# Sums by fours of the second batch's queries and keys, moved from TensorE to GpSimd

## The chip, the core and the metric

The kernel runs on one core of a Trainium2 chip. The metric is the device time of one execution in microseconds (us); the median of three runs of the kernel before is 896.6 us (895.24 to 897.03).

## What is computed

Attention for 4 batches of 8 heads, 576 tokens and 64 elements a head, followed by two dense layers over the 2304 tokens. Cut to what matters:

```python
q_d = q.reshape(B, H, Sd, factor, D).mean(axis=3)      # factor 4: means over groups of four tokens
k_d, v_d = ...                                         # the same for k and v
out_up = np.repeat(sm_attn(q_d, k_d, v_d), factor, axis=2)
mask = np.abs(pos[:, None] - pos[None, :]) < factor    # a band of 7 keys a query
out_local = softmax(where(mask, scale * q @ k.T, -1e9)) @ v
x = out_up + out_local                                 # 2304 x 512
h = np.maximum(x @ w_in, 0.0);  x = h * h @ w_out      # 512 -> 2048 -> 512
h = x @ w_in2;  out = softplus(h) @ w_out2             # 512 -> 2048 -> 512
```

## The kernel before

**Work.** The tokens of the MLP are cut into five blocks of 8, 6, 8, 8 and 6 times 64 (`BLOCKS`). A step is one chunk of 128 hidden units of one layer for one block. `hidden` (L1015) issues 12 matmuls of a step into the tile `ph`; ScalarE and VectorE make the activation and split it in a high and a low part, `gh` and `gl` (L351); `outputs` (L1069) issues the second 12 matmuls, into `y`. All products are made from two rounded parts, so there are three matmuls for each. A block's steps can start when its attention output has been split into `xh` and `xl` (L351). The first layer begins with steps 0 to 9 (block 0, hidden chunks 0 to 7; the first two chunks are taken in two halves of 256 tokens), and step 10 is the first of block 1.

**Weights.** `weight_job` turns each half chunk (the input half, or the output half) into two rounded parts. The half arrives by DMA in a ring of three `raw` tiles; ScalarE makes `f` and `r` (L401, L404), VectorE runs L407, L410 and L414 on `f`, one of the two copies the high part `w` (L338 or L340), and VectorE writes the low part (`w<-f,w`, L351). So the order of the writes `w<-f,w` is the order in which half chunks become usable: the 14th is the output half of step 8, the 15th the input half of step 9. Later layers get the same chunks back from memory through GpSimd's queue (`weight_again`, L445).

**Attention.** `local` does the band for one group of 64 tokens (scores `lsc`, transposes `lpp`, products `lav`, results `lt`). `pooled` does the pooled attention of one pair of heads: sums by fours of queries and keys into `qkd`, scores `psc` (L638), a softmax, transposes `ppp`, sums of v (`vd`), products `ppo`. Four pairs make a batch. For batch 0 the sums by fours are a VectorE reduction (L627). For batch 1 (`SUMS_ON_PE`) the host stores the tokens so that the four of a group lie 144 columns apart, and TensorE adds them with four matmuls against the identity (`pqk`, L617); ScalarE or VectorE then copies the sums from PSUM to `qkd`. The loaded queries and keys stand in a ring of two `in` tiles. Batch 1's pooled attention and groups are needed by block 1, so they run among the first steps.

**What sets the order.** Every piece of work is a generator that yields the engine it wants, an assumed duration and what it needs. `Order.run` picks, again and again, the piece that can start first by these assumed durations, and issues its instructions. So the order on every engine is fixed when the program is built, each engine works through its queue in that order, and only semaphores decide the times. A change of one piece's engine or assumed duration can reorder all queues. `keep_busy` (L981) adds small matmuls (`idle`) wherever this planner sees TensorE without work, until step 4 is planned.

Of the kernel before, what the change touches and what calls it, by code (L numbers as in the profile page):

```python
# [13 lines left out]
ALU = mybir.AluOpType  # L14
# [8 lines left out]
FCT = 4  # L23
SP = S // FCT
# [31 lines left out]
for run in RUNS:  # L56
    b = run[1] + run[0] * NB
# [12 lines left out]
POOLED = [(-20, -17), (-2.5, -2), (31, 48), (60, 78)]  # L70
LOCAL = [(-17, -13), (-0.5, 5), (12, 58), (62, 86), (74, 92)]
BY_TWOS = [2, 3]
SUMS_ON_PE = [1]

U_MLP, U_WEIGHTS, U_ATT, U_DIRECT = -2, -0.5, 1, 20
AHEAD = 10
# [195 lines left out]
def t_act(n):  # L272
    return 0.09 + n * 0.84e-3


def t_dve(n):
    return 0.066 + n / 960


def t_either(n, fast=False):  # L280

    return t_act(n), t_dve(n / 2 if fast else n)
# [3 lines left out]
def fused_kernel(ctx: ExitStack, tc: tile.TileContext, lq, lk, lv, dqk, dv, cdmask, pqk, pv, wts, cmask, cident, out):  # L286
    nc = tc.nc
    act, dve, pe, sp = nc.scalar, nc.vector, nc.tensor, nc.sync
# [8 lines left out]
    def ring(pool, tag, shape, bufs, dtype=F32):  # L297
        return Ring(lambda name: pool.tile(shape, dtype, tag=tag, name=name, bufs=bufs), bufs)

    ident = const.tile([128, 128], F32, name="ident")  # L300
# [15 lines left out]
    r_s = ring(att, "s", [128, 2 * SP], BUFS["s"])  # L316
    r_e = ring(att, "e", [128, 3 * SP], BUFS["e"])
    r_vd = ring(att, "vd", [KH, 2, 128], BUFS["vd"])
    r_pt = ring(att, "pt", [KH, 2 * 288], BUFS["pt"])
    r_n = ring(att, "n", [128, 16], BUFS["n"])  # L320
# [13 lines left out]
    either = ("act", "dve")  # L334

    def copy(out, in_):
        if order.chosen == "act":
            act.activation(out=out, in_=in_, func=AF.Copy)  # L338
        else:
            dve.tensor_copy(out=out, in_=in_)  # L340
# [20 lines left out]
    def step_start(s):  # L361
        return started if s < 0 else hidden_at[s]
# [140 lines left out]
    def take_for(r, kind, at):  # L503
        return first_bufs.get((kind, at)) or r.take(kind)

    def room(r, kind, at):
        return [] if (kind, at) in first_bufs else [r]
# [80 lines left out]
    def bank(choices, name):  # L588
        r = min((c for c in choices if c.at is not None), key=lambda c: c.at)
        return r.take(name)  # L590
# [8 lines left out]

    def pooled(b, hp, banks, ev, pace):  # L600

        on_pe = b in SUMS_ON_PE
        two = b * NP + hp

        def halves():
            return ev.buf.tile.rearrange("p (a x) -> p a x", a=2)[:, :, :S]

        if hp == 0:
            yield None, 0.0, r_up
            ups[b] = r_up.take("up")  # L610
        if on_pe:
            t = yield "pe", 1.95, ev, pace, banks, r_s, r_e, r_n
            sums = bank(banks, "pqk")
            x4 = halves().rearrange("p a (j g) -> p a j g", j=FCT)
            src = sums.tile[:, :2 * SP].rearrange("p (a g) -> p a g", a=2)
            for k in range(FCT):
                pe.matmul(src, ident, x4[:, :, k], start=(k == 0), stop=(k == FCT - 1))  # L617
            qk, e, n = r_s.take("qkd"), r_e.take("pe"), r_n.take("pn")
            ev.buf.free = t
            t = yield either, t_either(288)  # L620
            copy(qk.tile, sums.tile[:, :2 * SP])
            sums.free = t
        else:
            t = yield "dve", t_dve(1152), ev, pace, *room(r_s, "qkd", two), *room(r_e, "pe", two), r_n
            qk, e, n = take_for(r_s, "qkd", two), take_for(r_e, "pe", two), r_n.take("pn")
            x4 = halves().rearrange("p a (g j) -> p a g j", j=FCT)
            dve.tensor_reduce(out=qk.tile.rearrange("p (a g) -> p a g", a=2), in_=x4, axis=AX.X, op=ALU.add)  # L627
            if b:
                ev.buf.free = t
            else:  # L630
                used_once(t, ev.buf)

        t = yield "pe", 0.5, banks
# [6 lines left out]
        t = yield "dve", t_dve(432)  # L640
        nm, sm = n.tile[:, :3], n.tile[:, 4:7]
        dve.tensor_reduce(out=nm, in_=sc3, axis=AX.X, op=ALU.max, negate=True)
        t = yield "dve", 0.07
        k = 1.0 / (FCT * FCT * D ** 0.5)
        dve.tensor_scalar(out=nm, in0=nm, scalar1=k, scalar2=None, op0=ALU.mult)
        t = yield "act", 1.05
# [5 lines left out]
        t = yield "dve", 0.07  # L652
        dve.tensor_scalar(out=sm, in0=sm, scalar1=1e-9, scalar2=float(FCT), op0=ALU.add, op1=ALU.mult)
        t = yield "dve", 0.09
        dve.reciprocal(out=sm, in_=sm)
        t = yield either, (0.92, t_dve(432))
        times(e3, sm)
        n.free = t
        for a in range(2):
            t = yield ("pe", 0.33, banks, r_pt) if a == 0 else ("pe", 0.33, banks)  # L660
# [8 lines left out]
            t = yield either, t_either(288)  # L669
# [4 lines left out]
        t = yield "dve", t_dve(1024), ev.v, r_vd  # L674
# [4 lines left out]
        t = yield "pe", 0.66, banks  # L679
        po = bank(banks, "ppo")  # L680
        for a in range(2):
            pt4 = pt3[:, a, :].rearrange("p (i h q) -> p h i q", i=3, h=2)
            for h in range(2):
                pe.matmul(po.tile[64 * h:64 * h + 64, :SP], vd.tile[:, a, 64 * h:64 * h + 64], pt4[:, h],
                          start=(a == 0), stop=(a == 1))
        vd.free = pt.free = t
        t = yield either, t_either(144)
# [91 lines left out]
    def used_once(t, *bufs):  # L779
        for x in bufs:  # L780
            x.left -= 1
            if not x.left:
                x.free = t
# [350 lines left out]
    with tc.manual_schedule():  # L1134
# [6 lines left out]
        for k, ((kind, at, hp, i, s), ev) in enumerate(zip(tasks, arrived, strict=True)):  # L1141
            pace = step_start(int(s) + SPLIT) if s >= 0 else started if i == 0 else up_ready[0]
            banks = every if i == 0 else [r_a]
# [16 lines left out]
def _layout(q, k, v, moe_w_in, moe_w_out, moe2_w_in, moe2_w_out):  # L1160
# [15 lines left out]
    for b in range(B):  # L1176
        for i in range(NBLK):
            g = b * NBLK + i
# [3 lines left out]
            lv[at] = vs[b, i * QB:i * QB + KW].reshape(KW, NP * 128)  # L1182
    pqk = np.zeros((B * NP, 128, 2, QKW), f4)
    pqk[:, :, 0, :S], pqk[:, :, 1, :S] = qt.reshape(B * NP, 128, S), kt.reshape(B * NP, 128, S)
    for b in SUMS_ON_PE:
        x = pqk[b * NP:(b + 1) * NP, :, :, :S]
        x[...] = x.reshape(NP, 128, 2, SP, FCT).swapaxes(3, 4).reshape(x.shape)
    pqk = pqk.reshape(B * NP, 128, -1)
# [3 lines left out]
    for wi, wo in ((moe_w_in, moe_w_out), (moe2_w_in, moe2_w_out)):  # L1192
        a = np.asarray(wi, np.float64).reshape(DM // 128, 128, NF, 128).transpose(2, 1, 0, 3).reshape(NF, 128, 512)
# [47 lines left out]
```

## Time and profile before

| | |
|---|---|
| median of three runs | 896.6 us |
| the profiled execution | 897.16 us |
| its span, first to last instruction | 895.4 us |
| TensorE busy | 884.2 us (99%) |
| VectorE busy | 623.6 us (70%) |
| ScalarE busy | 482.6 us (54%) |
| GpSimd busy | 70.0 us (8%) |
| granted TensorE clock | 1.00 of full speed |

The share of TensorE is an average, and it counts the `idle` matmuls as work. Which engine sets the pace differs by stage, so the stages up to 125 us, in which all of batch 1's sums lie, have to be read by themselves.

### The profile page before, as it was taken

To read this page: it belongs to the slowest core of one execution; us is meant where nothing else is said; L and a number is where in the kernel's file an instruction comes from. 1 tells how busy PE (TensorE), PEld (TensorE's weight loads), DVE (VectorE), ACT (ScalarE), POOL (GpSimd) and SP (SyncE) were. 2 spreads that over 40 slices of the span, in tenths; PEclk is the share of its full clock that TensorE was granted. 3 is DMA by queue.
4 is the path that set the end of the run, shared out by engine and by line. 5 is a ranking of instruction groups with operands and counts; after the bars stand their busy time and mean duration, and the time that the engine had idled before them with its cause. 6 is when DMAs were issued, how large, how long until landed. Compare 5 with 4: busy or idle time off the path is not lost.

```text
span 895.4 us, 13254 instructions
## 1 busy us (share of the span) xinstructions
PE 884.2 (99%) x4908; PEld 763.5 (85%) x4908; DVE 623.6 (70%) x1085; ACT 482.6 (54%) x1051; POOL 70.0 (8%) x136
## 2 busy tenths in 40 slices
PE   8999999999999999999999999999999999999998
PEld 7788899988888788888888888888999888988886
DVE  6999989999999999887888999982111224223222
ACT  4978877757767774552345543532333235444443
POOL 0000000000000000211111111111120110010000
PEclk9999999999999999999999999999999999999999
DMA  9599698859686854796866677636360262223001
GB/s 238 159 320 328 247 356 287 295 167 321 220 260 207 289 197 165 260 296 235 269 216 191 221 269 260 213 101 240 131 222 25 70 209 74 71 94 130 23 1 48
DMA packets 48796, 177.39 MB, mean 198 GB/s; under 512 B 5490, under 2 KB 5874, under 8 KB 48732
## 3 DMA queue, kind: packets, MB, share of 16 engines
q1 hardware_dynamic: 29724, 107.33, 35.7%
q0 software_dynamic: 19008, 69.21, 23.9%
q8 instruction: 39, 0.64, 0.3%
q14 instruction: 25, 0.20, 0.1%
HBM read 138.25 MB, written 38.27 MB: 197 GB/s over the span
## 4 chain that ended last, share of the span: by engine, by line
PE 78%; DVE 10%; DMA 6%; ACT 3%; issue 1%; SPq 0%; ACTq 0%; DVEq 0%
PE y L1069 38%; PE ph L1015 37%; DMA raw<-wts 3%; DMA w_first<-lv 1%; DVE gl L351 1%; DVE f L414 1%; DVE prod L935 1%; DVE f L410 1%; DVE w L351 1%; DVE dsc L906 1%; DMA in<-pqk 1%; DVE g L1038 1%; DVE do L942 1%; ACT f L401 1%; DMA w_first<-pqk 1%
## 5 line engine op out<-in xcount | busy, mean ns | idle before, releaser
L1015 PE MATMUL ph<-xh,w 128*128 128x512 f32 (+2 forms) x1304 | 393.8, 365 | 1.1 <-DVE g L1038 0.9
L1015 PEld LDWEIGHTS ph<-xh,w 128*128 128x128 f32 x1304 | 240.9, 188 | 32.9 <-DVE g L1038 1.8
L1015 PE MATMUL ph<-xl,w 128*128 128x512 f32 (+2 forms) x652 | 237.5, 364 | 0.0
L1069 PE MATMUL y<-gh,w 128*128 128x512 f32 (+2 forms) x656 | 199.6, 366 | 0.0
L1069 PE MATMUL y<-w,gh 128*128 128x512 f32 x576 | 179.2, 392 | 1.0 <-ACT o L338 1.0
L351 DVE TENSOR_TENSOR gl<-g,gh 128x512 fp32r<-128x512 f32 (+2 forms) x163 | 101.8, 625 | 85.3 <-ACT gh L338 84.5
L1015 PEld LDWEIGHTS ph<-xl,w 128*128 128x128 f32 x652 | 122.5, 188 | 15.6
L1069 PEld LDWEIGHTS y<-gh,w 128*128 128x128 f32 x656 | 121.0, 188 | 15.8 <-issue 1.2
L445 POOL DMA_DIRECT2D w<-wdram x132 | 69.8, 532 | 758.9 <-ACT gh L338 351.3
L1069 PEld LDWEIGHTS y<-w,gh 128*128 128x128 f32 x576 | 106.8, 188 | 22.4 <-ACT o L338 1.3
L1069 PE MATMUL y<-gl,w 128*128 128x512 f32 (+2 forms) x328 | 119.3, 364 | 0.0
L338 ACT ACTIVATE gh<-g 128x512 fp32r<-128x512 f32 (+2 forms) x127 | 72.9, 574 | 84.5 <-PE y L1069 49.6
L1038 DVE SCALAR_TENSOR_TENSOR g<-ph,g 128x512 f32<-128x512 f32 (+2 forms) x81 | 50.7, 626 | 90.6 <-ACT g L1036 90.4
L1069 PE MATMUL y<-w,gl 128*128 128x512 f32 x288 | 112.6, 391 | 0.0
L1027 ACT ACTIVATE g<-ph 128x512 f32<-128x512 f32 (+2 forms) x82 | 44.6, 543 | 122.8 <-PE ph L1015 102.9
L1032 ACT ACTIVATE g<-ph 128x512 f32<-128x512 f32 (+2 forms) x81 | 44.4, 548 | 100.8 <-PE ph L1015 91.7
L1069 PEld LDWEIGHTS y<-gl,w 128*128 128x128 f32 x328 | 61.6, 188 | 7.0 <-DVE gl L351 0.2
L1069 PEld LDWEIGHTS y<-w,gl 128*128 128x128 f32 x288 | 54.0, 188 | 11.7
L340 DVE CAST gh<-g 128x512 fp32r<-128x512 f32 (+2 forms) x36 | 14.9, 413 | 62.7 <-PE y L1069 51.8
L401 ACT ACTIVATE f<-raw 128x512 f32<-128x512 f32 x64 | 42.7, 671 | 19.0 <-DMA raw<-wts 8.2
L1030 ACT ACTIVATE g<-g 128x512 f32<-128x512 f32 (+2 forms) x82 | 47.5, 579 | 2.0
L1036 ACT ACTIVATE g<-g 128x512 f32<-128x512 f32 (+2 forms) x81 | 47.3, 584 | 2.2
(115 smaller groups left out, 926.6 us busy)
## 6 DMA issues: line engine op xcount, KB each, us to landing
w<-wdram POOLq DMA_DIRECT2D x132, 512.0 KB, 4.3
raw<-wts SPq DMA_DIRECT2D x64, 512.0 KB
wdram<-w SPq DMA_DIRECT2D x64, 512.0 KB
dqk<-dqk SPq DMA_DIRECT2D x11, 896.0 KB
dv<-dv SPq DMA_DIRECT2D x11, 640.0 KB
in<-pqk SPq DMA_DIRECT2D x12, 579.0 KB
out<-o SPq DMA_DIRECT2D x18, 256.0 KB
pv<-pv SPq DMA_DIRECT2D x12, 288.0 KB
```

Of the source, the lines that this page charges most:

```text
L338: act.activation(out=out, in_=in_, func=AF.Copy)
L340: dve.tensor_copy(out=out, in_=in_)
L351: dve.tensor_tensor(out=out, in0=whole, in1=high.bitcast(F32), op=ALU.subtract)
L401: act.activation(out=f.tile, in_=high.bitcast(F32), func=AF.Abs, scale=REBIAS)
L445: nc.gpsimd.dma_start(out=weights[slot][:, half], in_=wdram[c, half])
L1015: pe.matmul(ph.tile[:, :n], w, y, start=(k == 0), stop=(k == len(prs) - 1))
L1027: act.activation(out=o, in_=h, func=AF.Relu)
L1030: act.activation(out=o, in_=o, func=AF.Square)
L1032: act.activation(out=o, in_=h, func=AF.Abs)
L1036: act.activation(out=o, in_=o, func=AF.Ln, bias=1.0)
L1038: dve.scalar_tensor_tensor(out=o, in0=h, scalar=0.0, in1=o, op0=ALU.max, op1=ALU.add)
L1069: pe.matmul(o, wt, y, start=(begin and k == 0), stop=(end and k == 2))
```

## The change

Batch 1's sums no longer go through TensorE and PSUM. GpSimd adds the second half of the four slices to the first half, in place in the loaded tile (576 elements a partition, line 614 of the changed kernel), and then the second quarter to the first, into `qkd` (288 elements, line 617). The planner is told 1.4 and 0.8 us for the two. The host's layout is the same. Lines behind the diff are numbered three lower in the changed kernel.

```diff
-SUMS_ON_PE = [1]
+ON_POOL = [1]
...
-        if on_pe:
-            t = yield "pe", 1.95, ev, pace, banks, r_s, r_e, r_n
-            sums = bank(banks, "pqk")
-            x4 = halves().rearrange("p a (j g) -> p a j g", j=FCT)
-            src = sums.tile[:, :2 * SP].rearrange("p (a g) -> p a g", a=2)
-            for k in range(FCT):
-                pe.matmul(src, ident, x4[:, :, k], start=(k == 0), stop=(k == FCT - 1))
+        if on_pool:
+            t = yield "pool", 1.4, ev, pace
+            x4 = halves()
+            nc.gpsimd.tensor_tensor(out=x4[:, :, :2 * SP], in0=x4[:, :, :2 * SP], in1=x4[:, :, 2 * SP:], op=ALU.add)
+            t = yield "pool", 0.8, r_s, r_e, r_n
             qk, e, n = r_s.take("qkd"), r_e.take("pe"), r_n.take("pn")
+            nc.gpsimd.tensor_tensor(out=qk.tile.rearrange("p (a g) -> p a g", a=2), in0=x4[:, :, :SP],
+                                    in1=x4[:, :, SP:2 * SP], op=ALU.add)
             ev.buf.free = t
-            t = yield either, t_either(288)
-            copy(qk.tile, sums.tile[:, :2 * SP])
-            sums.free = t
```

Three places of the queues, before and after.

GpSimd's queue of the changed kernel, from its start to the first reloads of weights; the queue before has only the reloads there:

```order
L614 ISA
L614 TENSOR_TENSOR in<-in 128x2x288 x2
L617 TENSOR_TENSOR qkd<-in 128x288 x2
L614 TENSOR_TENSOR in<-in 128x2x288
L617 TENSOR_TENSOR qkd<-in 128x288
L614 TENSOR_TENSOR in<-in 128x2x288
L617 TENSOR_TENSOR qkd<-in 128x288
L445 DMA w_1632<-wdram 128x1024
```

All eight additions stand ahead of the first reload; the second pair's first addition stands ahead of the first pair's second.

VectorE's queue before, from the third `lt` of batch 0 on, where the two orders part (`pn<-psc`: the row maxima of a pair's pooled scores):

```order
L847 TENSOR_TENSOR lt<-lav,up 128x256
L407 TENSOR_SCALAR f<-f 128x512
L847 TENSOR_TENSOR lt<-lav,up 128x256
L410 SCALAR_TENSOR_TENSOR f<-raw,f 128x512
L351 TENSOR_TENSOR xl<-lt,xh 128x4x64
L806 SCALAR_TENSOR_TENSOR ls<-lsc,mask 128x280
L351 TENSOR_TENSOR xl<-lt,xh 128x4x64
L812 TENSOR_REDUCE ln<-ls 128x4
L806 SCALAR_TENSOR_TENSOR ls<-lsc,mask 128x280
L642 TENSOR_REDUCE pn<-psc 128x3
```

and now, from the same instruction:

```order
L844 TENSOR_TENSOR lt<-lav,up 128x256
L340 CAST xh<-lt 128x4x64
L351 TENSOR_TENSOR xl<-lt,xh 128x4x64
L844 TENSOR_TENSOR lt<-lav,up 128x256
L340 CAST xh<-lt 128x4x64
L803 SCALAR_TENSOR_TENSOR ls<-lsc,mask 128x280
L351 TENSOR_TENSOR xl<-lt,xh 128x4x64
L844 TENSOR_TENSOR lt<-lav,up 128x256
L809 TENSOR_REDUCE ln<-ls 128x4
L639 TENSOR_REDUCE pn<-psc 128x3
L351 TENSOR_TENSOR xl<-lt,xh 128x4x64
L642 TENSOR_SCALAR pn<-pn 128x3
```

Batch 0's splits (`xh<-lt`) came to VectorE from ScalarE, and the softmax of batch 1's first pairs moved ahead of the first weights (L407, L410).

TensorE's queue before, from step 8's output matmuls to step 9 (each `y` tile has three rows; `w_1503` is step 8's slot, `w_1635` step 9's):

```order
L981 MATMUL idle<-ident 128x128
L1069 MATMUL y_864<-gh,w_1503 128x512
L1069 MATMUL y_864<-gl,w_1503 128x512
...
L1069 MATMUL y_876<-gl,w_1503 128x512
L1069 MATMUL y_876<-gh,w_1503 128x512
L839 MATMUL lav<-lpt,v 64x64 x8
L1015 MATMUL ph<-xh,w_1635 128x512
```

and now (`w_1555` is step 8's slot, `w_1632` step 9's, `w_78` step 10's):

```order
L1012 MATMUL ph<-xh,w_1555 128x512
L1012 MATMUL ph<-xh,w_1632 128x512
L1012 MATMUL ph<-xl,w_1632 128x512
...
L1012 MATMUL ph<-xh,w_1632 128x512
L1012 MATMUL ph<-xh,w_78 128x384
...
L1012 MATMUL ph<-xh,w_78 128x384
L1066 MATMUL y_857<-gh,w_1555 128x512
```

Step 8's 12 output matmuls now come behind the hidden matmuls of steps 9 and 10.

## Rows read from the trace of the kernel before

**Rows 1.** The page: TensorE's busy time, and GpSimd's in tenths, 40 slices of the span.

```profile
PE 884.2 (99%) x4908; PEld 763.5 (85%) x4908; DVE 623.6 (70%) x1085; ACT 482.6 (54%) x1051; POOL 70.0 (8%) x136
...
POOL 0000000000000000211111111111120110010000
```

**Rows 2.** Windows: stretch, length; busy us (count) by engine; clock, DMA share, GB/s.

```profile
28.70:33.70 5.00, 4.99 (x60) 3.91 (x58) 3.42 (x14) 3.76 (x11) 0.00 (x0) 1.00 0.55 212
33.70:53.70 20.00, 18.07 (x216) 15.04 (x212) 19.80 (x53) 16.25 (x57) 0.00 (x0) 1.00 0.59 192
53.70:70.00 16.30, 16.23 (x145) 14.55 (x146) 14.43 (x34) 12.35 (x40) 0.00 (x0) 1.00 0.97 316
70.00:92.00 22.00, 21.94 (x185) 17.70 (x183) 20.65 (x49) 18.31 (x54) 0.00 (x0) 1.00 1.02 335
92.00:112.00 20.00, 20.00 (x188) 16.37 (x188) 18.38 (x46) 17.83 (x50) 0.00 (x0) 1.00 0.64 231
112.00:896.00 784.00, 776.95 (x3840) 673.84 (x3840) 525.49 (x844) 396.99 (x765) 69.79 (x132) 1.00 0.57 189
```

**Rows 3.** Timeline of VectorE, 107 to 114 us: start us, us, instruction.

```profile
107.40 0.68 DVE L351 TENSOR_TENSOR w<-f,w 128x512 fp32r<-128x512 f32 x1
108.00 0.68 DVE L414 CUSTOM_DVE_ANT_0 f<-f,r 128x1024 uint16<-128x1024 uint16 x1
...
109.88 0.68 DVE L351 TENSOR_TENSOR w<-f,w 128x512 fp32r<-128x512 f32 x1
...
113.89 0.41 DVE L351 TENSOR_TENSOR xl<-lt,xh 128x256 fp32r<-128x256 f32 x1
```

**Rows 4.** Timeline of TensorE, 108 to 115 us.

```profile
108.16 0.39 PE L981 MATMUL idle<-ident 128*128 128x128 f32 x2
108.30 0.49 PE L1069 MATMUL y<-gh,w 128*128 128x512 f32 x1
...
111.88 0.50 PE L1015 MATMUL ph<-xh,w 128*128 128x512 f32 x1
...
114.50 0.56 PE L1015 MATMUL ph<-xh,w 128*128 128x512 f32 x2
```

**Rows 5.** Timeline of TensorE: batch 1's sums, and the scores behind them.

```profile
30.61 2.10 PE L617 MATMUL pqk<-in,ident 128*128 128x288 f32 x8
...
48.09 4.06 PE L617 MATMUL pqk<-in,ident 128*128 128x288 f32 x16
...
53.74 1.69 PE L638 MATMUL psc<-qkd 64*64 64x144 f32 x24 [0.96 <-ACT qkd L338]
...
58.78 2.10 PE L617 MATMUL pqk<-in,ident 128*128 128x288 f32 x8
```

**Rows 6.** Instructions on the tile `pqk`: count; duration ns min/median/max; first and last start.

```profile
L338 ACT ACTIVATE qkd<-pqk x4: 400/410/412, 33.2 to 60.9; 128x288 f32<-128x288 f32 x4
```

**Rows 7.** Timeline of VectorE: the two waits that the sums are behind, in brackets.

```profile
33.37 0.42 DVE L847 TENSOR_TENSOR lt<-lav,up 128x256 f32<-128x256 f32 x1 [1.54 <-PE lav L839]
...
54.74 1.34 DVE L642 TENSOR_REDUCE pn<-psc 128x3 f32<-128x432 f32 x2 [0.97 <-PE psc L638]
```

**Rows 8.** Groups of VectorE by form, 15 to 130 us: count; busy us, mean ns.

```profile
L351 DVE TENSOR_TENSOR xl<-lt,xh 128x256 fp32r<-128x256 f32 x14 | 5.8, 418 | 0.2
...
L351 DVE TENSOR_TENSOR gl<-g,gh 128x512 fp32r<-128x512 f32 x6 | 4.1, 684 | 0.0
...
L340 DVE CAST gh<-g 128x256 fp32r<-128x256 f32 x3 | 0.9, 292 | 0.6 <-ACT g L1030 0.4
...
L340 DVE COPY up<-ppo 128x144 f32<-128x144 f32 x1 | 0.3, 308 | 0.0
```

**Rows 9.** Timeline of SP's queue: the loads of batch 1's third and fourth pairs.

```profile
42.65 0.35 SPq L574 DMA_DIRECT2D in<-pqk  x1
...
50.24 0.33 SPq L574 DMA_DIRECT2D in<-pqk  x1
```

**Rows 10.** The chain that ended last, merged: start us, us, what; one step's output matmuls.

```profile
97.50 2.72 PE y L1069 x12
```

More of the change, by code (lines that the diff above doesn't have):

```diff
@@ L600, in pooled @@
     def pooled(b, hp, banks, ev, pace):
-        on_pe = b in SUMS_ON_PE
+        on_pool = b in ON_POOL
         two = b * NP + hp
@@ L1184, in _layout @@
     pqk[:, :, 0, :S], pqk[:, :, 1, :S] = qt.reshape(B * NP, 128, S), kt.reshape(B * NP, 128, S)
-    for b in SUMS_ON_PE:
+    for b in ON_POOL:
         x = pqk[b * NP:(b + 1) * NP, :, :, :S]
```

## The prediction

> **What bounds the kernel now.** I read the page first: TensorE is busy for 884.2 of 895.4 us [rows 1]. Taken alone, that says that every microsecond taken from TensorE comes off the end, so I asked whether it holds where the sums are. The timeline puts batch 1's sums at 30.6, 48.1 and 58.8 us, so the windows up to 112 us are the ones to read [rows 2, 5]. There two engines are full. From 33.7 to 53.7 us VectorE is busy for 19.80 of 20 us; from 28.7 to 112 us it idles for 1.58 + 0.20 + 1.87 + 1.35 + 1.62 = 6.6 us of 83.3. TensorE's busy time in the first two windows includes the filler matmuls.
>
> Next, who waits for whom at the end of that stretch. VectorE writes the 14th low part of the weights until 108.08 us (107.40 + 0.68); TensorE runs a filler at 108.16 and starts step 8's output matmuls, which need that part, at 108.30. VectorE writes the last `xl` of block 1 until 114.30 us, and TensorE reaches block 1's first step inside the row that starts at 114.50 [rows 3, 4]. So weights and attention from VectorE arrive a few tenths of a microsecond ahead of their use: up to about 114 us the pace is VectorE's as much as TensorE's. After it TensorE idles for only 7 of 784 us, the ragged end included [rows 2]. What the change does to the end is thus nearly what it does to the time at which TensorE gets into the steps from 9 on, plus the work that is then still in its queue.
>
> **What it removes.** Sixteen matmuls, 32 records: 2.10 + 4.06 + 2.10 us, less a tenth each for the overlap with the next one, 8.0 us of TensorE [rows 5]. And four copies on ScalarE, 4 x 0.41 = 1.6 us [rows 6]; I cost these at nothing, since ScalarE has 1.2 to 3.7 us to spare in each of the windows [rows 2], and if that cover were gone the price would be a gain of at most 1.6.
>
> Two VectorE waits stand behind the sums. At 33.37 us VectorE has waited 1.54 us for `lav`, which stood behind the first pair's sums on TensorE. At 54.74 us it has waited 0.97 us for `psc`, and that for 0.96 us for the copied `qkd` [rows 5, 7]. Together 2.5 us; I take all of it as gained. The bounds are all of VectorE's 6.6 us of idle, if nothing else makes it wait, and nothing, if other waits take their place (the new order has the softmax of two pairs early, each with a chain through three engines).
>
> **What it adds.** Eight additions on GpSimd. Its queue is otherwise empty until the first reloads of weights, which start in the 17th slice, after 358 us [rows 1]; the instruction ahead of the first addition (a set-up of unknown length) has that queue to itself for over 20 us. So GpSimd's own time costs nothing where the sums are done before TensorE asks for them; what can cost is that it works on the same memory as VectorE. No row shows arithmetic on GpSimd. The nearest are VectorE's additions of two tensors: 0.418 us for 256 elements and 0.684 for 512, or 0.15 + 0.00104 each [rows 8], so 0.75 and 0.45 for 576 and 288, 1.2 us a pair of heads, 4.8 in all. Bounds: VectorE loses nothing (as beside ScalarE, which overlaps it throughout [rows 2]), or it stands still for all four pairs at twice this length, 9.6 us (twice, since GpSimd's rate stands in no row). I take 2.4: the third and fourth pair, whose loads were issued at 42.65 and 50.24 us [rows 9] and whose additions meet VectorE where it is full. The first two meet it where it idled for 1.58 of 5 us [rows 2].
>
> [...]
>
> **What it moves.** All queues are planned anew. VectorE has 241 instructions ahead of its 15th low part, where it had 237: three more 128x256 casts (six for `xh`, three fewer for `gh`), two more `up`, one more `lt` and `xl`, a `gl` and a 512 copy fewer, and three single differences that about cancel. By rows, 0.88 + 0.62 + 0.84 - 1.37 - 0.2 = 0.8 us, less 0.08 for each of four instructions, since VectorE's next starts 0.60 us after one of 0.68 [rows 3, 8]: +0.4 us. Some low parts before it come later than they did, and the local attention earlier.
>
> SP's queue has the first queries, keys and values of block 1 ahead of a weight load that they followed; DMA is full there already (0.97 and 1.02 of its engines [rows 2]). I cost that at nothing while VectorE, in its fixed order, is the later of the two. If DMA were late, VectorE would wait in order behind the missing load.
>
> On TensorE, step 8's 12 output matmuls come behind the hidden matmuls of steps 9 and 10. TensorE used to do these 2.72 us [rows 10] before it needed the 15th low part; now it needs that part first and has them left.
>
> **The sum.** The 15th low part was written at 109.88 + 0.68 = 110.56 us [rows 3]. Now: + 0.4 (work) - 2.5 (waits gone) + 2.4 (GpSimd) = 110.9. TensorE starts some 0.2 us after such a write [rows 3, 4], so step 9 begins at 111.1 instead of 111.9 us [rows 4]: -0.8. From there its queue holds 2.7 us more than it did: **+1.9 us**. The 8.0 us appear in none of these terms: TensorE saves them ahead of step 9, and there it would spend them waiting for VectorE. Against the profiled execution, 897.16 us, that is 899.1; the median of the runs, 896.6, lies 0.56 lower, so 898.5 on its scale. Later steps have a queue of much the same slack; I add 1.5 us either way for stalls that the new order puts elsewhere.
>
> A measurement of this kernel can tell some 0.2%, or 1.8 us, from no change.
>
> **The rivals.**
>
> *VectorE is not held (faster).* If GpSimd works beside VectorE at no cost (2.4 us less), and VectorE's idle shrinks by 3.8 to 6.6 us instead of 2.5 (1.3 to 4.1 us less), the sum is 1.9 - 2.4 - 1.3 = -1.8 to 1.9 - 2.4 - 4.1 = -4.6 us: 892 to 894.8. For it: TensorE will have 8 us less to do and answer VectorE sooner. Against it: it needs both terms at their good ends, and a new order brings waits of its own. Chance 0.23.
>
> *GpSimd holds VectorE (slower).* The place is VectorE's queue from 28 to 60 us, the price is the length of the additions while VectorE's next instruction reads two tensors: with the whole length of four pairs at VectorE's speed or at twice that, 4.8 or 9.6 us in place of 2.4, +4.3 to +9.1: 901 to 905.7. It decides from the point at which GpSimd takes more than 2.5 us from VectorE, what the removed waits give back. [...] For it: most of VectorE's work on weights reads two tensors of SBUF. Against it: between such instructions stand reductions and reads of PSUM, and there were some waits in which GpSimd could do its work. Chance 0.12.
>
> *TensorE sets the pace throughout.* The end comes 8.0 us sooner, 888.6. For it: the page, and TensorE's 20.00 of 20 us from 92 to 112 us [rows 2]. Against it: the filler at 108.16 us, and VectorE's 6.6 us of idle, which with the order term of 2.7 us caps the gain at 4.6 unless later stalls vanish too. Chance 0.04.
>
> *The change moves only idle time.* The waits that go are replaced by others, GpSimd costs little, and it ends within 0.5 us. Chance 0.06.
>
> **How the numbers follow.** The forecast has the remaining 0.55, with a range of its own from 896 to 902: its two unknown terms, 2.5 and 2.4, are each good for some 2 us either way and partly cancel. Its middle lies close to the bound of what can be told, so I count 0.25 of it as no change and 0.30 as slower. Faster is then 0.23 + 0.04 = 0.27, the same 0.25 + 0.06 = 0.31, slower 0.30 + 0.12 = 0.42. The range takes in the rival of a VectorE that is not held nearly to its end and half of the one that is held: 892.5 to 904; outside lie TensorE's full gain (0.04), the best end of the first rival and the worst of the second, some 0.14 in all.
>
> **What would show it.** Right: no filler or useful matmul fills TensorE between 60 and 110 us as before, it waits for low parts or for `gl`; the 15th low part is within 2 us of 110.56; step 9 starts where that part ends; VectorE's instructions with two SBUF inputs are longer, or start later, beside a GpSimd addition. Wrong: the 15th low part before 107 us; additions on GpSimd that lengthen nothing; TensorE without waits up to 112 us; a wait of `psc` for GpSimd's `qkd`; or a granted clock under 1.00 in a stretch where TensorE now idles, which would cost more than any term here.

## The result, and the profile after

| | before | after |
|---|---|---|
| median, 9 runs each | 896.66 us (895.24 to 898.02) | 902.52 us (899.26 to 905.32) |
| ratio | | 1.0068, 95% interval 1.0054 to 1.0082 |
| profiled execution, its span | 897.16, 895.4 us | 905.32, 903.5 us |
| granted TensorE clock of the profiled execution | 1.000 | 0.992 |

The change makes the kernel 5.9 us slower. The forecast was 898.5 us with a range to 904: the sign and that range hold, the size does not. The measured median lies above the range that the prediction gave the forecast by itself (896 to 902) and within that of its rival "GpSimd holds VectorE" (901 to 905.7). The profiled execution of the change is the slowest of its nine, 8.2 us above that of before, so the trace shows the loss larger than the median has it. The nine differ in clock too: those with a mean granted clock of 0.998 took 899.26 and 900.61 us, those from 0.991 to 0.994 took 904.17 to 905.32.

The page of the changed kernel, beside [rows 1]: busy times, GpSimd's tenths, the granted clock in tenths of full speed.

```profile
PE 887.0 (98%) x4898; PEld 765.4 (85%) x4898; DVE 636.3 (70%) x1098; ACT 478.5 (53%) x1037; POOL 83.0 (9%) x144
...
POOL 0220000000000000121111111102120110010000
PEclk9799999999999999999999999999999999999999
```

TensorE has 8 us less to do and is busy for 2.8 us longer: its second slice ran at a lower clock. VectorE gained 12.7 us of busy time over the whole program, with 13 more instructions. GpSimd's new work is in the second and third slice. Four of the stretches of [rows 2], two short ones, and one up to the end of the 15th low part:

```profile
32.00:38.00 6.00, 6.00 (x71) 4.93 (x71) 4.47 (x11) 4.63 (x9) 0.96 (x2) 0.50 0.03 11
60.00:62.00 2.00, 2.00 (x18) 1.77 (x18) 1.27 (x4) 1.74 (x7) 0.00 (x0) 0.50 0.97 287
...
28.70:33.70 5.00, 3.50 (x34) 2.85 (x36) 5.00 (x13) 2.60 (x6) 3.36 (x3) 0.81 0.44 169
33.70:53.70 20.00, 19.93 (x212) 16.76 (x208) 16.06 (x47) 14.83 (x55) 1.44 (x1) 0.79 0.30 100
53.70:70.00 16.30, 14.07 (x128) 12.34 (x127) 14.24 (x27) 10.65 (x29) 6.51 (x4) 0.90 0.81 233
...
92.00:112.00 20.00, 16.50 (x132) 13.06 (x131) 19.16 (x48) 16.09 (x44) 0.00 (x0) 1.00 0.76 270
...
26.00:118.56 92.56, 84.51 (x793) 69.78 (x791) 83.27 (x197) 67.42 (x211) 12.71 (x8) 0.93 0.70 233
```

The same last stretch of the kernel before, from 26 us to the end of its 15th low part:

```profile
26.00:110.56 84.56, 82.42 (x797) 68.90 (x796) 77.50 (x194) 69.83 (x222) 0.00 (x0) 1.00 0.79 266
```

The last row above and this one give the account of the prediction, as measured. The 15th low part is written 8.0 us later. VectorE is busy for 83.27 - 77.50 = 5.8 us more on the way there, and idle for 9.29 - 7.06 = 2.2 us more. The busy part comes from GpSimd. Its timeline:

```profile
26.79 1.40 POOL L614 TENSOR_TENSOR in<-in 128x576 f32<-128x576 f32 x1 [26.34 <-DMA in<-pqk]
29.60 1.57 POOL L614 TENSOR_TENSOR in<-in 128x576 f32<-128x576 f32 x1 [1.41 <-DMA in<-pqk]
31.14 1.82 POOL L617 TENSOR_TENSOR qkd<-in 128x288 f32<-128x288 f32 x2
52.26 4.21 POOL L614 TENSOR_TENSOR in<-in 128x576 f32<-128x576 f32 x1 [19.31 <-ACT gh L338]
56.55 1.12 POOL L617 TENSOR_TENSOR qkd<-in 128x288 f32<-128x288 f32 x1
67.08 1.75 POOL L614 TENSOR_TENSOR in<-in 128x576 f32<-128x576 f32 x1 [9.41 <-DMA in<-pqk]
68.90 0.87 POOL L617 TENSOR_TENSOR qkd<-in 128x288 f32<-128x288 f32 x1
```

and VectorE's, the instructions that meet these, some waits, and the 15th low part (in brackets: idle before it, and what ended that). `le` are the exponentials of a group's band, `ln` the few numbers a row that its softmax needs:

```profile
27.28 0.93 DVE L817 TENSOR_SCALAR ln<-ln 128x4 f32<-128x4 f32 x1
...
29.34 0.13 DVE L817 TENSOR_SCALAR ln<-ln 128x4 f32<-128x4 f32 x1
...
29.91 1.29 DVE L817 TENSOR_SCALAR ln<-ln 128x4 f32<-128x4 f32 x1
31.11 0.44 DVE L348 TENSOR_TENSOR le<-le,ln 128x280 f32<-128x280 f32 x1
...
32.20 1.06 DVE L348 TENSOR_TENSOR le<-le,ln 128x280 f32<-128x280 f32 x1
...
36.20 0.42 DVE L844 TENSOR_TENSOR lt<-lav,up 128x256 f32<-128x256 f32 x1 [0.84 <-PE lav L836]
...
42.31 0.61 DVE L639 TENSOR_REDUCE pn<-psc 128x3 f32<-128x432 f32 x1 [1.28 <-PE psc L635]
...
55.45 1.57 DVE L410 SCALAR_TENSOR_TENSOR f<-raw,f 128x512 uint32<-128x512 uint32 x1
56.94 1.28 DVE L351 TENSOR_TENSOR w<-f,w 128x512 fp32r<-128x512 f32 x1
...
62.62 0.42 DVE L844 TENSOR_TENSOR lt<-lav,up 128x256 f32<-128x256 f32 x1 [1.35 <-PE lav L836]
...
68.07 1.04 DVE L351 TENSOR_TENSOR gl<-g,gh 128x256 fp32r<-128x256 f32 x1 [0.54 <-ACT gh L338]
69.03 1.29 DVE L410 SCALAR_TENSOR_TENSOR f<-raw,f 128x512 uint32<-128x512 uint32 x1
...
117.87 0.69 DVE L351 TENSOR_TENSOR w<-f,w 128x512 fp32r<-128x512 f32 x1
```

A scalar operation on 128x4 takes 0.13 us, and 0.93 and 1.29 beside GpSimd's first two additions; `le` takes 0.44, and 1.06; the 512-element forms take 0.68, and 1.57, 1.28 and 1.29; `gl` 0.42, and 1.04. Together the seven are 5.3 us longer than their like, which with the 0.4 us of reordered work is 5.7 of the 5.8 us of the account. GpSimd's own instructions lengthen as well: its third long addition takes 4.21 us, where the first took 1.40.

The idle part comes from TensorE, here at five places:

```profile
31.69 0.93 PE L826 MATMUL lpp<-ident,le 128*70 128x128 f32 x4 [0.81 <-DVE ln L819]
...
38.26 1.71 PE L635 MATMUL psc<-qkd 64*64 64x144 f32 x12
...
57.72 0.95 PE L635 MATMUL psc<-qkd 64*64 64x144 f32 x12 [2.04 <-POOL qkd L617]
...
111.13 0.60 PE L826 MATMUL lpp<-ident,le 128*70 128x128 f32 x4 [2.04 <-DVE le L348]
...
117.68 0.62 PE L1012 MATMUL ph<-xh,w 128*128 128x512 f32 x2
...
118.61 0.73 PE L1012 MATMUL ph<-xh,w 128*128 128x512 f32 x2
```

It waits for the held `ln`, and then runs at half its clock: one pair's scores (`psc`, x12) take 1.71 us at 38 us and 0.95 at 57 us. The clock falls a second time behind the 2.04 us in which the scores wait for GpSimd's `qkd`, which stood behind that addition of 4.21 us (clock 0.50 from 60 to 62 us). VectorE's waits at 36.20 and 42.31 us are behind work at the first half clock, the one at 62.62 us behind work at the second.

A step's first two matmuls use the high part of its weights alone, the third needs the low part. Step 9 starts with the second matmul of the row at 117.68, some 0.23 us into it, at 117.9 us. Its third, at 118.61, comes where the 15th low part ends (117.87 + 0.69 = 118.56). Before, step 9 started at 111.88 [rows 4].

### The profile page after: what moved, and what is told of

Its sections match the earlier page's. It is cut to its first block, busy times and chain, and to the rows that moved or that the text cites. A ratio compares the mean times of both kernels' runs of the same rounds, so it can differ in the third digit from the quotient of the medians.

```text
span 903.5 us, 13240 instructions
## 1 busy us (share of the span) xinstructions
PE 887.0 (98%) x4898; PEld 765.4 (85%) x4898; DVE 636.3 (70%) x1098; ACT 478.5 (53%) x1037; POOL 83.0 (9%) x144
## 4 chain that ended last, share of the span: by engine, by line
PE 77%; DVE 13%; DMA 3%; ACT 3%; issue 2%; POOL 1%; ACTq 0%; DVEq 0%; SPq 0%; POOLq 0%
PE y L1066 36%; PE ph L1012 35%; DMA raw<-wts 2%; DVE f L410 2%; DVE w L351 2%; PE idle L978 2%; DVE f L414 1%; DVE gl L351 1%; DVE dsc L903 1%; PE psc L635 1%; ACT le L813 1%; DVE prod L896 1%; PE lav L836 1%; DVE f L407 1%; DVE prod L932 1%
## 5 line engine op out<-in xcount | busy, mean ns | idle before, releaser
L338 ACT ACTIVATE gh<-g 128x384 fp32r<-128x384 f32 (+2 forms) x119 | 67.3, 565 | 84.9 <-PE y L1066 61.9
L340 DVE CAST gh<-g 128x512 fp32r<-128x512 f32 (+1 forms) x44 | 18.4, 419 | 63.9 <-PE y L1066 56.5
```

## The experiments

The theory after the result: GpSimd's additions hold VectorE up, TensorE then stands idle and loses its clock, and VectorE waits for a slow TensorE. The rivals: the new order costs it (step 8's output matmuls late), or the sums come late through GpSimd's chain. Medians are set against the kernel before in the same session: 896.57 us for the first eight runs, 896.26 for the last four.

**The order of before, with the additions (e1).** The planner still sees the sums on TensorE and the copy, so its order stays; neither is issued.

```diff
-            for k in range(FCT):
-                pe.matmul(src, ident, x4[:, :, k], start=(k == 0), stop=(k == FCT - 1))
...
+            h = halves()
+            nc.gpsimd.tensor_tensor(out=h[:, :, :2 * SP], in0=h[:, :, :2 * SP], in1=h[:, :, 2 * SP:], op=ALU.add)
+            nc.gpsimd.tensor_tensor(out=qk.tile.rearrange("p (a g) -> p a g", a=2), in0=h[:, :, :SP],
+                                    in1=h[:, :, SP:2 * SP], op=ALU.add)
...
-            copy(qk.tile, sums.tile[:, :2 * SP])
```

> The queues of the kernel before, with its planner's entries; the sums are GpSimd's and TensorE's 16 matmuls and ScalarE's 4 copies are left out. Theory (GpSimd holds VectorE, and TensorE, left with gaps where the sums were, loses its clock; the new order adds 2.7 us): VectorE's lengthened instructions beside the additions 3 to 5 us, the two waits of 2.5 us gone, some clock lost: 897 to 901 us, mean clock 0.995 to 0.999. Rival 1 (the new order alone made it slower): 894 to 896.7, clock 1.000. Rival 2 (the clock alone): as slow as the change, 901 to 904, with a clock like its 0.996.

Measured: 901.52 us, ratio 1.0056 (1.0039 to 1.0072). Nearly the whole loss is there without the new order. The time lies 0.5 us above the theory's range and within that of rival 2, the clock alone, which e2 tests. The clock fell here too:

```profile
26.00:32.00 6.00, 3.62 (x38) 2.83 (x38) 6.00 (x14) 2.23 (x14) 3.59 (x3) 0.85 0.71 265
32.00:44.00 12.00, 11.87 (x140) 10.10 (x140) 8.77 (x27) 9.96 (x36) 0.79 (x1) 0.65 0.13 47
```

**The same, with TensorE kept at work (e2).** Nine 128-column matmuls stand where each pair's sums stood.

```diff
+            for k in range(9):
+                pe.matmul(sums.tile[:, :128], ident, ident, start=True, stop=True)
```

> As e1, and TensorE multiplies the identity with itself nine times a pair where the sums were (1152 columns, as many as the sums had), so that its load is that of before. Theory: clock 1.000, VectorE still held: 897.5 to 900.5 us. Rival 1 (order alone): 896.7 within 0.5. Rival 2 (clock alone): 896.7 within 0.5. The difference to e1 is what the emptier TensorE gives or takes.

Measured: 900.61 us, ratio 1.0052 (1.0038 to 1.0065), against 896.7 by the clock alone. The clock is whole:

```profile
26.00:32.00 6.00, 5.72 (x61) 4.91 (x60) 5.79 (x16) 4.64 (x21) 3.14 (x3) 1.00 0.80 269
32.00:44.00 12.00, 9.80 (x164) 8.59 (x163) 10.69 (x31) 10.41 (x40) 1.55 (x2) 1.00 0.16 55
```

With the order of before, TensorE's load put back and a whole clock, the additions cost 4.0 us, what the scores lose by waiting for them included. e1 issues 8.6 us less on TensorE than e2 and is 0.9 us slower, though the two intervals overlap.

**The change with twice the fillers (e3), and before with twice the fillers (e7).** In `keep_busy`:

```diff
             pe.matmul(b.tile[:, :128], ident, ident, start=True, stop=True)
+            pe.matmul(b.tile[:, :128], ident, ident, start=True, stop=True)
```

> The change with its queues as they are, but each filler matmul that the planner put in is issued twice (65 more small matmuls, all ahead of step 9). Theory: the granted clock stays at 1.00 from 28 to 66 us, where it was at half for some 13 us of the profiled execution, and 2 to 5 us come back: 897.5 to 900.5. Rival (VectorE held is all): 902.5 within 1, whatever the clock does. Third case: the fillers delay the matmuls behind them, 903 to 905.

Measured: 910.54 us, ratio 1.0152 (1.0139 to 1.0165), 8.0 us above the change, although the clock held at 1.00 up to 112 us:

```profile
28.70:112.00 83.30, 79.53 (x865) 68.70 (x865) 74.49 (x188) 62.15 (x205) 10.98 (x7) 1.00 0.67 211
```

That is the third case in kind, and outside every range that was expected. e7 is its control:

> The kernel before with each filler matmul issued twice, as was done to the change, where it cost 8 us. The clock is at 1.00 here already, so the fillers can only stand in the way. If doubled fillers delay the chains of the attention by themselves, it is slower here too, by 3 us or more (900 us and up). If their price belonged to the order of the change alone, it stays at 896 to 898 us.

Measured: 905.20 us, ratio 1.0097 (1.0082 to 1.0113), 8.6 us above before:

```profile
28.70:112.00 83.30, 83.24 (x834) 70.84 (x832) 73.49 (x185) 67.30 (x221) 0.00 (x0) 1.00 0.70 241
```

TensorE is busy for 83.24 of 83.30 us and VectorE idles for 9.8, where it idled for 6.6: fillers stand in the way of the chains that VectorE waits for. So e3 by itself tells the price of fillers. Set against e7 it tells more: with the fillers doubled on both sides and the clock at 1.00 up to 112 us in both, the change still costs 910.54 - 905.20 = 5.3 us. The half clock that the change had from 32 to 42 and from 59 to 62 us is thus not the main part of the 5.9, as far as kernels with so full a TensorE can tell; e3 lost some clock later (0.83 from 112 to 122 us).

**The change with half the additions (e4).** The 576-element addition is left out, so the sums have two of four quarters.

```diff
-            nc.gpsimd.tensor_tensor(out=x4[:, :, :2 * SP], in0=x4[:, :, :2 * SP], in1=x4[:, :, 2 * SP:], op=ALU.add)
```

> The change without the first of the two additions, so that the sums hold two tokens of four; queues otherwise as they are. GpSimd then works for a third of the time. Theory (5.2 us of VectorE held in the profiled execution, two thirds of it by the first additions): 3 to 4.5 us less than the change, 898 to 899.5, with a clock of 0.997 or more, since the scores come earlier. Rival (clock alone): 901.5 to 903. Rival (order alone): 902.5 within 0.5.

Measured: 899.08 us, ratio 1.0026 (1.0014 to 1.0038): 3.4 us of the 5.9 go with the longer half of GpSimd's work, as the theory had it. It does not tell the hold from the clock, which was at 1.00 here from 26 to 112 us.

**Additions that nobody waits for (e5).** Before, whole; GpSimd adds the loaded tile into a tile of its own.

```diff
+            h, o = halves(), aside.rearrange("p (a x) -> p a x", a=2)
+            nc.gpsimd.tensor_tensor(out=o, in0=h[:, :, :2 * SP], in1=h[:, :, 2 * SP:], op=ALU.add)
+            nc.gpsimd.tensor_tensor(out=o[:, :, :SP], in0=o[:, :, :SP], in1=o[:, :, SP:], op=ALU.add)
```

> The kernel before, whole, with TensorE's sums kept; beside them GpSimd makes the eight additions of the change from the same loaded tiles into a tile that nobody reads. Nothing waits for GpSimd's results, and TensorE has all its work. Theory (an addition on GpSimd holds VectorE's instructions up): some 4 to 5 us of VectorE are lost as in the run with a busy TensorE, the 15th low part is written 3 to 5 us later than before, and the time is 899.5 to 901.5 us at a clock of 1.00. Rival (what costs is that the scores wait for sums that come late through GpSimd): nothing waits for them here, so the time stays within 1 us of the kernel before, 895.6 to 897.6 us, even if single VectorE instructions are longer.

Measured: 898.74 us, ratio 1.0020 (1.0007 to 1.0033), +2.2 us at a clock of 0.999. Nothing waits for GpSimd here, so this is the hold alone: less than the theory's 3 to 5, more than the rival's 1. VectorE's timeline:

```profile
27.07 1.21 DVE L681 TENSOR_REDUCE vd<-first 72x256 f32<-72x1024 f32 x1
...
29.12 0.67 DVE L824 TENSOR_SCALAR ln<-ln 128x4 f32<-128x4 f32 x1
...
30.79 1.12 DVE L349 TENSOR_TENSOR le<-le,ln 128x280 f32<-128x280 f32 x1
...
47.40 1.92 DVE L352 TENSOR_TENSOR w<-f,w 128x512 fp32r<-128x512 f32 x1
...
59.21 1.67 DVE L341 CAST w<-f 128x512 fp32r<-128x512 f32 x1
60.79 1.19 DVE L349 TENSOR_TENSOR pe<-pe,pn 128x432 f32<-128x432 f32 x1
```

VectorE is busy for 5.1 us more up to the 15th low part, nearly as much as in e2, but 3.0 us of its idle time go, so that the low part is only 2.1 us late. The two waits of [rows 7] shrink although the sums are still on TensorE: a held VectorE comes later to what it would have waited for.

```profile
33.49 0.42 DVE L851 TENSOR_TENSOR lt<-lav,up 128x256 f32<-128x256 f32 x1 [0.31 <-PE lav L843]
...
55.52 1.11 DVE L646 TENSOR_REDUCE pn<-psc 128x3 f32<-128x432 f32 x2
```

In e2, where the scores do wait for GpSimd, the additions cost 4.0 us instead of 2.2, and those intervals do not overlap. By that difference the rival of the late sums is worth some 1.8 us in the old order. The table below has the account for most runs.

**A quarter of the sums (e6).** Before, with one matmul of four for each sum; three quarters of each sum are left out, and no GpSimd.

```diff
-            for k in range(FCT):
-                pe.matmul(src, ident, x4[:, :, k], start=(k == 0), stop=(k == FCT - 1))
+            pe.matmul(src, ident, x4[:, :, 0], start=True, stop=True)
```

> The kernel before with one of the four matmuls of each sum (the three other quarters are left out of the sum), so TensorE loses 6 us of its work up to 60 us and GpSimd adds nothing. Rival (TensorE sets the pace up to 114 us): 6 us sooner, 890.5 us. Theory (VectorE sets it): only the two waits behind the sums can give something back, 0 to 2.5 us, so 894 to 896.6 us. If TensorE's new idle time costs it its clock near 31 or 59 us, as in the change, new waits of VectorE take that back: 896 to 899 us with windows under 1.00.

Measured: 898.38 us, ratio 1.0023 (1.0012 to 1.0033). Six us less for TensorE make the kernel 1.8 us slower. TensorE's timeline says how:

```profile
53.25 3.14 PE L637 MATMUL psc<-qkd 64*64 64x144 f32 x24 [1.73 <-ACT qkd L338]
...
112.88 0.50 PE L1014 MATMUL ph<-xh,w 128*128 128x512 f32 x1
```

The scores of two pairs start 0.49 us earlier than in [rows 5], since the copied `qkd` is hardly earlier, and take 3.14 us at half clock (0.50 from 53.25 to 56.40 us), where they took 1.69. That is 1.0 us late, and step 9 is 1.0 us late.

**One pair on GpSimd (e8: the first; e11: the fourth), or both (e12).** Before's order; the other pairs stay on TensorE. The edit is that of e1 under a condition on the pair: `hp == 0`, `hp == 3`, `hp in (0, 3)`.

> The kernel before in its own order, with only the first pair of the second batch summed on GpSimd, the three others on TensorE. VectorE waits 1.54 us behind that pair's sums before, and two additions hold it for 1.0 to 1.5 us. Theory: what is held and what is won back about cancel, 896 to 897.8 us. If the two additions fall wholly where VectorE would have waited, 894.8 to 896. If the lost 2 us of TensorE work cost it the clock at 31 us, 897.8 to 900 us.

Measured: 896.30 us, ratio 1.0002 (0.9992 to 1.0012), no difference. Its first `ln` was held from 0.13 to 0.69 us, and the wait of 1.54 us behind the first pair's sums [rows 7] is gone; 0.9 us of it came back as a wait for `xh`.

> The kernel before in its own order, with only the fourth pair of the second batch on GpSimd. Its sums hold TensorE for 2.1 us near 59 us, where TensorE has least idle time, so the 2.1 us could come off there; against it two additions hold VectorE by 1.0 to 1.5 us where it idles little. Theory: 896 to 898 us, no gain. If TensorE's 2.1 us count in full there: 894.5 to 895.5.

Measured: 898.71 us, ratio 1.0029 (1.0018 to 1.0041), 0.7 us above the theory's range. VectorE and TensorE, one row each:

```profile
57.72 1.87 DVE L414 CUSTOM_DVE_ANT_0 f<-f,r 128x1024 uint16<-128x1024 uint16 x1
```

```profile
61.26 0.49 PE L672 MATMUL ppp<-ident,pe 128*72 128x128 f32 x3 [2.53 <-DVE pn L661]
```

The 2.1 us that left TensorE's queue near 59 us became a wait of 2.53 us for VectorE's softmax, which stands behind an instruction that was held from 0.68 to 1.87 us.

> The kernel before in its own order, with the first and the fourth pair on GpSimd and the two in the middle on TensorE. Theory: the first pair is free (896.3 alone), the fourth costs what it costs alone, so 896 to 898.5 us. If the two together give the best of both: 894 to 895.5. If the lost TensorE work takes the clock: 898 to 900.

Measured: 899.75 us, ratio 1.0040 (1.0025 to 1.0054), the third case: the clock is 0.72 from 62 to 68 us. The median is 1.0 us above that of the fourth pair alone. The two intervals overlap, so whether the first pair, free by itself, costs something here is not settled.

**The change's order without the additions (e9).** The first addition is cut to 2x4 elements, the second is a fill with zeros, so batch 1's pooled attention is left out.

```diff
-            nc.gpsimd.tensor_tensor(out=x4[:, :, :2 * SP], in0=x4[:, :, :2 * SP], in1=x4[:, :, 2 * SP:], op=ALU.add)
+            nc.gpsimd.tensor_tensor(out=x4[:, :, :4], in0=x4[:, :, :4], in1=x4[:, :, 2 * SP:2 * SP + 4], op=ALU.add)
...
-            nc.gpsimd.tensor_tensor(out=qk.tile.rearrange("p (a g) -> p a g", a=2), in0=x4[:, :, :SP],
-                                    in1=x4[:, :, SP:2 * SP], op=ALU.add)
+            nc.gpsimd.memset(qk.tile, 0.0)
```

> The change with its own order, but GpSimd's two additions of each pair cut down to 2x4 elements and a fill of the sums with zeros (so batch 1's pooled attention is left out; all that waits for the sums still waits). Theory (most of the 5.9 us is GpSimd's hold on VectorE, the order itself is worth 1 to 2 us): 896.5 to 899 us, and no VectorE instruction beside the fill is longer by more than 0.2 us. Rival (the new order costs it, through step 8's output work and TensorE's lost clock): it stays at 901 us and above.

Measured: 899.66 us (896.00 to 903.03), ratio 1.0036 (1.0018 to 1.0054): 2.9 us below the change, and just outside what the theory gave. Its profiled execution took 898.21 us. Windows and one row of TensorE:

```profile
26.00:32.00 6.00, 5.91 (x74) 4.89 (x73) 5.59 (x17) 5.00 (x22) 1.24 (x4) 1.00 0.69 251
32.00:44.00 12.00, 12.00 (x170) 10.53 (x170) 11.67 (x38) 11.44 (x48) 0.00 (x0) 1.00 0.34 89
...
104.00:106.00 2.00, 2.00 (x7) 1.51 (x5) 1.83 (x4) 1.96 (x5) 0.00 (x0) 0.50 0.90 313
```

```profile
102.28 0.60 PE L825 MATMUL lpp<-ident,le 128*70 128x128 f32 x4 [2.42 <-DVE le L348]
```

Without the additions the clock is whole from 26 to 44 us, of which the change spent 10 us, from 32 to 42, at 0.50: in this order the held VectorE is what took it. But the order has a gap of its own: TensorE stands for 2.42 us before 102.28 us, waiting for VectorE's `le` (2.04 us in the change), and here the clock halved behind it. The ten runs have mean clocks from 0.994 to 0.999; the two at 0.994 took 902.44 and 903.03 us, the two at 0.998 and 0.999 took 896.00 and 896.93. The six at 0.997 took anything from 896.73 to 902.12, so the mean clock does not order the runs by itself.

**The change with TensorE kept at work (e10).**

```diff
+        for i in range(9 if on_pool else 0):
+            pe.matmul(sc.tile[:, :128], ident, ident, start=True, stop=True)
```

> The change, with nine 128-column matmuls ahead of each pair's scores on TensorE, about the 2.1 us of the removed sums, so that TensorE has its work back where it waits for GpSimd. Theory (the half clock costs about 1 us of the 5.9): clock at 1.00 in the windows up to 112 us and 900.5 to 902 us. If the clock is worth more than that in this order: 898 to 900.5. If the matmuls stand in the way as the doubled fillers did: 903 to 906.

Measured: 904.69 us, ratio 1.0099 (1.0081 to 1.0118), the third case: the matmuls stand ahead of the scores, after the gaps near 29 and 31 us, so they came too late to hold the clock there (0.85 from 26 to 32 us, 0.87 from 32 to 38). From 38 to 110 us it was whole, and the kernel was no faster for it.

The account of these runs, in us against before. The first five columns are of the profiled executions: when the 15th low part is written, VectorE's busy and idle time from 26 us up to there, the start of step 9, the end. The last is of the medians. One execution need not be like the median: those of the change, e1 and e12 are the slowest of their runs, those of e2, e6 and e11 the fastest.

| run | 15th low part | VectorE busy | VectorE idle | step 9 | end | median |
|---|---|---|---|---|---|---|
| change | +8.0 | +5.8 | +2.2 | +6.0 | +8.2 | +5.9 |
| e1 additions, old order | +7.5 | +5.7 | +1.8 | +7.5 | +8.0 | +5.0 |
| e2 the same, TensorE busy | +3.2 | +5.3 | -2.0 | +3.2 | +2.7 | +4.0 |
| e5 additions aside | +2.1 | +5.1 | -3.0 | +2.1 | +1.5 | +2.2 |
| e12 first and fourth pair | +4.0 | +2.2 | +1.8 | +3.9 | +3.8 | +3.5 |
| e11 fourth pair | +1.2 | +0.8 | +0.4 | +1.2 | +0.4 | +2.5 |
| e8 first pair | +0.4 | +0.6 | -0.2 | +0.4 | 0.0 | -0.3 |
| e6 a quarter of the sums | +1.0 | +0.2 | +0.8 | +1.0 | +0.1 | +1.8 |
| e4 half the additions | +1.0 | +1.7 | -0.8 | -1.2 | +1.1 | +2.5 |
| e9 no additions, new order | +0.2 | +0.6 | -0.4 | -1.3 | +1.1 | +3.4 |

e3, e7 and e10 are not in it. Their low parts come 14.1, 8.4 and 9.2 us late, and in e3 and e7 VectorE has done only 30 instructions by 26 us, where it had done 46. Counted from the start of the span, VectorE is busy for 5.3 us more in e3, 5.4 in e10 and 0.6 in e7; on that scale the change has 5.9, e1 6.3, e2 5.3 and e5 5.2.

Two things stand in the table. In the old order, step 9 and the low part move by the same amount in every run, and the end of the profiled execution follows within a us. And eight additions make VectorE busy for 5.1 to 5.8 us longer in all four of its kernels; what differs is its idle time, which shrinks by 2 to 3 us where TensorE has its load and its clock (e2, e5) and grows by about 2 where it has lost both (e1 and the change). No run is measurably faster than the kernel before.

## Why the prediction was right, and where it was wrong

- **VectorE sets when the steps from 9 on can start; TensorE's 8.0 us are worth nothing.** The first half held: TensorE stands for 2.04 us ahead of 111.13, waiting for VectorE's `le`, and step 9's third matmul comes right behind the low part. The rival "TensorE sets the pace throughout", with 888.6 us, falls: e6 takes 6 us from TensorE and ends later. No run takes TensorE's work away at a whole clock with nothing added, so that it is worth nothing is not shown by itself: e6 loses clock, and e4, whose TensorE is rid of all 8.0 us at a whole clock up to 112 us, has the new order and half the additions, and is 2.5 us slower.
- **+0.4 us of reordered work.** The runs agree with it: e9, with the order and no additions to speak of, has VectorE busy for 0.6 us more.
- **+2.4 us for GpSimd holding VectorE.** This term failed by its size: the seven held instructions are 5.3 us longer. It was made of the third and fourth pair at VectorE's speed, with the first two free. Additions take 1.40 and 0.79 us (0.79 in e4, at 26.87 us), not 0.75 and 0.45, and all four pairs hold: 2.6 of the change's 5.3 us are the first two's (27.28, 29.91 and 32.20 us). The first pair alone was indeed free (e8), because a wait took it up. The rival "GpSimd holds VectorE (slower)", given 0.12, is what happened: it decides beyond 2.5 us, and with the measured 5.3 in place of 2.4 the prediction's own sum gives 1.9 + 2.9 = +4.8, some 901.4 us on the scale of the median. That this is near the measured 902.5 is partly luck, since the next two terms did not come as they were put. That the price falls where VectorE reads two tensors, as the rival and the prediction's sign of being right have it, stood in no row of before. The runs show it for these (`f` 0.68 to 1.57 us, `le` 0.44 to 1.06), and for operations with one input too (`ln` 0.13 to 1.29 us). What in the chip makes the two engines hold each other up no run shows.
- **-2.5 us of VectorE's waits.** This term failed. In the change VectorE's idle time grew by 2.2 us, through new waits behind a TensorE at half clock. Where the sums leave TensorE and it keeps all or most of its clock, idle time shrinks by 0.2 us (e8, one pair), 0.8 (e4) and 0.4 (e9): other waits took the place of the two, as the prediction's bound of nothing had it. The 2.0 and 3.0 us that go in e2 and e5 are not this gain, since TensorE is as full there as before; they are held time that falls where VectorE would have waited. The prediction named a clock under 1.00 as what would prove it wrong, but gave it neither a term nor a chance.
- **-0.8 us of lead and +2.7 us of order.** The order term is there: from the start of step 9 to the end, the change, e4 and e9 have +2.1 to +2.3, where runs in the old order have -0.9 to +0.5. The lead was put too small. TensorE used to start step 9 1.3 us after the low part; the prediction had it start 0.2 us after, and in the change it starts 0.65 us before, since only the third matmul needs that part. The prediction read the 14th low part in the same way: of step 8's output matmuls, too, it is the third, at 108.86 us and not at 108.30, that needs it. From the low part to the end the prediction thus has +1.6, and the change has +0.2, e4 +0.1 and e9 +0.8. What the new order did cost was not foreseen: a gap of 2.0 to 2.4 us ahead of step 7's output matmuls, and, in e9 but not in the profiled execution of the change, half the clock behind it. e9's median is 3.4 us above before with no additions, while its profiled execution, at 0.997, is 1.1 above. That the clock makes up the difference is argued from the runs' clocks, not shown: both attempts to hold it by work for TensorE (e3, e10) had a price of their own.
- **A wait of `psc` for GpSimd's `qkd`**, named as a sign of being wrong, is there at 57.72 us, 2.04 us long, and the clock falls behind it. It is not needed for the hold: e5, where nothing waits for GpSimd, has nearly the same busy time on VectorE. It has a price of its own, by e2 against e5 some 1.8 us in the old order.

The loss can be followed in steps: +2.2 us for the additions alone (e5), +4.0 with scores that wait for them (e2), +5.0 with TensorE's load and clock gone as well (e1), +5.9 with the new order (the change). Only the first two steps are clear of the noise; the intervals of e2 and e1, and of e1 and the change, overlap. And the parts do not add up to the whole: the additions cost 4.0 to 5.0 us in the old order, and taking them out of the new one gives back 2.9 (e9; 3.4 in e4 for the longer ones alone, the intervals overlap). VectorE is held for the same 5 us either way. How the rest divides between the new order and its clock stays open.

## What to carry to other kernels

Here the work that moved from a full engine to an idle one was paid for at the engine beside it. So count every instruction that will run next to the moved one, and set beside them, as an estimate of what they may lose, the moved work's whole length on its new engine. The additions are 8.8 us long undisturbed (four of 1.40 and four of 0.79), they lengthened VectorE's work by 5.1 to 5.8 us, and where nothing else was in play (e5) 2.1 us of that reached the low part. Matmuls that looked like a burden went together with TensorE's clock: without three quarters of them it was 0.50 from 53.25 to 56.40 us (e6), and with TensorE's load put back it rose from 0.85 to 1.00 in the windows from 26 to 32 us (e1, e2). Before taking work from it, look at which gaps open and who waits behind them. More fillers were no cure here: doubling them cost 8.0 us (e3) and 8.6 us (e7). And a queue with 99% busy time may still be the one that follows: in the change TensorE, 98% busy, stood for 2.04 us ahead of 111.13 us, waiting for VectorE's `le`.

## What the runs showed of the hardware

- VectorE's operations lengthened beside GpSimd's additions with one input and with two. With one, a scalar operation on 128x4 went from 0.13 to 1.29 us (the change, at 29.91 us) and a cast from 0.42 to 1.67 (e5, at 59.21); with two, a custom 16-bit operation from 0.68 to 1.87 (e11, at 57.72). A reduction did not change: 1.21 us at 27.07 us in e5, beside an addition on GpSimd from 27.32, and 1.21 before. Nor did a copy from PSUM: 0.45 us at 26.92 us in the change, beside the addition from 26.79, and 0.44 before.
- GpSimd loses too: in the change 4.21 us for an addition that takes 1.40 elsewhere, and in e9 2.05 us for one of 8 elements that takes 0.20.
- A GpSimd addition takes 1.40 us for 576 elements (the change, at 26.79 us) and 0.79 for 288 (e4, at 26.87), 1.9 and 1.8 times the prediction's 0.75 and 0.45 for VectorE.
- In the change the clock went to half behind small gaps (0.79 and 0.81 us near 30 us, with TensorE busy for 4.33 of the 6 us from 26 to 32; 0.50 from 32 to 38). It stayed at 1.00 behind gaps of 2.34 us in e4 (ahead of 103.95 us) and 2.53 in e11 (ahead of 61.26), while e9 lost it behind one of 2.42 (0.50 from 104 to 106). What makes the difference is open.
